# Random-feature attention and a low-rank mixer on one core: moving the weight loads, transposing the first tiles on TensorE, and pinning the order of loads

## The chip, the cores and the metric

The kernel runs on one core of a Trainium2 chip. The metric is the device time of one execution in microseconds (us). "Span" is the time from the first to the last instruction in a profiled execution; it is about 2 us shorter than the device time of the same execution. An execution counts as slow when it is over 1.5% above the fastest of the same kernel in its list, else as fast; ratios use fast ones alone.

## The reference, cut to what matters

Eight batches, eight heads, 576 positions, head size 64. Queries and keys are projected on 128 random directions; cosine and sine of the projections are the features. The attention is linear in those features. Its output x goes through a low-rank mix over the positions and then through a two-layer MLP of width 2048.

```python
def phi(x):
    proj = np.einsum('bhsd,md->bhsm', x, omega)
    return np.concatenate([np.cos(proj), np.sin(proj)], axis=-1) / np.sqrt(m)
kv  = np.einsum('bhsm,bhsd->bhmd', phi(k), v);  z = phi(k).sum(axis=2)
num = np.einsum('bhsm,bhmd->bhsd', phi(q), kv); den = np.einsum('bhsm,bhm->bhs', phi(q), z)
x   = num / den                                   # heads side by side: (8, 576, 512)
u   = x + (x.transpose(0, 2, 1) @ U @ V).transpose(0, 2, 1)
out = u + np.maximum(u @ w_ch1, 0) @ w_ch2
```

## The kernel before

Work is cut into 16 quads of four heads. A quad's k and q are loaded as bf16 by GpSimd's DMA queue, transposed by DMA on SyncE's queue, and used as two groups of two heads. A step s of the main loop emits the angles of group s, the key-values and numerators of group s-1, and one quarter of an MLP batch, six steps behind. A scheduler then places the instructions on the engines, a list for each. One point carries most of this study: an instruction that waits holds up those behind it on the same engine (in e8 below, a load on GpSimd that waits 6.7 us holds up the add behind it, and ScalarE with it).

A batch's 576 positions are four tiles of 128 and 64 left over. The leftovers of two batches, a pair, share one tile and are worked on together as the pair's tail, so the run has four pairs.

```python
    def load_quad(n, parts=1, veng=nc.sync):
        for name, src in (("k", k), ("q", q)):
            raw[name, n] = rawp.tile([P, 2, NS * D], BF16, name=f"{name}raw")
        vraw = rawp.tile([P, 2, NS * D], F32, name="vraw")
        # ... the k and q loads on nc.gpsimd, in parts
        veng.dma_start(vraw, quad(v, n))
        nc.gpsimd.tensor_copy(vq[n % NV][:, :, 0:D], vraw.rearrange("p i (s d) -> p (i s) d", d=D))
    # transpose_quad(n): nc.sync.dma_start_transpose(tpos[...], raw[...]) for k and q

    def angles(g):
        # ... TensorE: pk, pt, pq; VectorE turns them to integer angles `ang`
        for a in range(2):
            nc.scalar.activation(out=ft[:, 0, a, :], in_=low[:, a, :, 0], func=ACT.Sin, scale=TO_RAD)
            nc.gpsimd.tensor_scalar(out=ang[:, a, :], in0=ang[:, a, :], scalar1=TURN / 4.0,
                                    scalar2=1.0, op0=ALU.add, op1=ALU.mult)
        for a in range(2):
            nc.scalar.activation(out=ft[:, 1, a, :], in_=low[:, a, :, 0], func=ACT.Sin, scale=TO_RAD)
    # ... key_values(g), numerators(g); token_mix(b): hu, hn, u, then a DMA transpose u -> uT
    # ... channel_in: h_ps = W1 x uT, hid = relu(h_ps) on ScalarE; channel_out: ch_ps = hid x W2

    load_quad(0, parts=2, veng=nc.scalar)
    transpose_quad(0, parts=2)
    load_quad(1, veng=nc.scalar)
    load_low_rank()
    for a in range(4):
        load_w1(a)                      # 4 x 1 MB of HBM, on GpSimd's queue
    for s in range(NG + 6):
        if s % 2 == 0:
            n = s // 2
            if n + 2 < NG // 2:
                load_quad(n + 2)
            if n + 1 < NG // 2:
                transpose_quad(n + 1)
        if s == 1:
            for a in range(4):
                load_w2(a)
        if s < NG:
            angles(s)
        if 0 <= s - 1 < NG:
            key_values(s - 1)
            numerators(s - 1)
            if (s - 1) % 4 == 3:
                token_mix((s - 1) // 4)
        if s >= 6:
            b, mc = divmod(s - 6, 4)
            if b < B:
                mlp_chunk(b, mc)
```

`ang`: GpSimd's "quarter-turn add" on it turns the angle of a sine into that of a cosine, and the second pair of ScalarE activations waits for it.

Of the kernel before, what the change touches and what calls it, by code (L numbers as in the profile page):

```python
# [20 lines left out]
R = 32  # L21
# [18 lines left out]
TO_RAD = float(np.nextafter(np.float32(np.pi / 32768.0), np.float32(0.0)))  # L40


@with_exitstack
def kernel(
    ctx: ExitStack,
# [13 lines left out]
    const = ctx.enter_context(tc.tile_pool(name="const", bufs=1))  # L59
    stage = ctx.enter_context(tc.tile_pool(name="stage", bufs=1))  # L60
    rawp = ctx.enter_context(tc.tile_pool(name="rawp", bufs=2))
    tposp = ctx.enter_context(tc.tile_pool(name="tposp", bufs=2))
    angp = ctx.enter_context(tc.tile_pool(name="angp", bufs=3))
    featp = ctx.enter_context(tc.tile_pool(name="featp", bufs=3))
    kvp = ctx.enter_context(tc.tile_pool(name="kvp", bufs=2))
    xp = ctx.enter_context(tc.tile_pool(name="xp", bufs=2))
    up = ctx.enter_context(tc.tile_pool(name="up", bufs=2))
    hidp = ctx.enter_context(tc.tile_pool(name="hidp", bufs=2))
    outp = ctx.enter_context(tc.tile_pool(name="outp", bufs=3))
    smallp = ctx.enter_context(tc.tile_pool(name="smallp", bufs=4))  # L70
    psum = ctx.enter_context(tc.tile_pool(name="psum", bufs=2, space=bass.MemoryType.PSUM))


    ident = const.tile([P, P], BF16, name="ident")
    make_identity(nc, ident)
    om_f = stage.tile([P, 2, D], F32, name="om_f")
    nc.sync.dma_start(om_f, omega.unsqueeze(1).to_broadcast([P, 2, D]))
    om_b = stage.tile([P, 2, D], BF16, name="om_b")
    nc.vector.tensor_copy(om_b, om_f)
    wt_ps = psum.tile([P, P], BF16, name="wt_ps", tag="at")  # L80
    nc.tensor.transpose(wt_ps, om_b, ident)
    WT = const.tile([P, M], BF16, name="WT")
    nc.vector.tensor_copy(WT, wt_ps)

    Ub = const.tile([P, NT, R], BF16, name="Ub")
    Ut = const.tile([P, R], BF16, name="Ut")
    Vb = const.tile([P, S], BF16, name="Vb")

    def load_low_rank():
        U_f = stage.tile([P, NT + 1, R], F32, name="U_f")  # L90
        U9 = moe_U.rearrange("(p s) r -> p s r", s=NS)
        for e in range(2):
            r = slice(e * TL, (e + 1) * TL)
            nc.scalar.dma_start(U_f[r, 0:NT, :], U9[:, e:2 * NT:2, :])
            nc.scalar.dma_start(U_f[r, NT, :], U9[:, 8, :])
        nc.any.tensor_copy(Ub, U_f[:, 0:NT, :])
        nc.any.tensor_copy(Ut, U_f[:, NT, :])
        Vf = stage.tile([P, S], F32, name="Vf")
        for g in range(4):
            nc.scalar.dma_start(Vf[g * R:(g + 1) * R, :], moe_V)  # L100
        nc.any.tensor_copy(Vb.rearrange("r (s p) -> r s p", p=TL), Vf.rearrange("r (p s) -> r s p", s=NS))

    W1b = const.tile([P, 4, NCT, 512], BF16, name="W1b")
    W2b = const.tile([P, NFT, C], BF16, name="W2b")

    def load_w1(a):
        nc.gpsimd.dma_start(W1b[:, a, :, :],
                            moe_w_ch1[:, a * 512:(a + 1) * 512].rearrange("(c p) f -> p c f", p=P))

    def load_w2(a):  # L110
        nc.gpsimd.dma_start(W2b[:, 4 * a:4 * a + 4, :],
                            moe_w_ch2[a * 512:(a + 1) * 512, :].rearrange("(f p) c -> p f c", p=P))

    def w1(ct, f):
        return W1b[:, f // 4, ct, f % 4 * P:(f % 4 + 1) * P]
# [3 lines left out]
    for i in range(NV):  # L119
        a = const.tile([P, 2 * NS, D + 1], BF16, name=f"vq{i}")  # L120
        nc.vector.memset(a[:, :, D:D + 1], 1.0)
        vq.append(a)


    raw, tpos = {}, {}

    def quad(src, n):
        b, h0 = n // 2, 4 * (n % 2)
        return src[b, h0:h0 + 4, :, :].rearrange("(i e) (p s) d -> (e p) i (s d)", e=2, s=NS)

    def load_quad(n, parts=1, veng=nc.sync):
        for name, src in (("k", k), ("q", q)):
            raw[name, n] = rawp.tile([P, 2, NS * D], BF16, name=f"{name}raw")
        vraw = rawp.tile([P, 2, NS * D], F32, name="vraw")
        for i in range(parts):
            w = slice(i * 2 // parts, (i + 1) * 2 // parts)
            for name, src in (("k", k), ("q", q)):
                nc.gpsimd.dma_start(raw[name, n][:, w, :], quad(src, n)[:, w, :])  # L138
        veng.dma_start(vraw, quad(v, n))
        nc.gpsimd.tensor_copy(vq[n % NV][:, :, 0:D], vraw.rearrange("p i (s d) -> p (i s) d", d=D))  # L140

    def transpose_quad(n, parts=1):
        for name in ("k", "q"):
            tpos[name, n] = tposp.tile([P, NS, P], BF16, name=f"{name}T")
        cut = [0, NS] if parts == 1 else [0, 5, NS]
        for a, e in zip(cut, cut[1:]):
            for name in ("k", "q"):
                src = raw[name, n].rearrange("p i e -> p (i e)")
                nc.sync.dma_start_transpose(tpos[name, n][:, a:e, :], src[:, a * P:e * P])


    st, x_of = {}, {}
# [43 lines left out]
    def key_values(g):  # L196
        n, i = divmod(g, 2)
        ft = st[g]
        kv_ps = psum.tile([P, 2, 512], F32, name="kv_ps", tag="mm" if g < 4 else "at")
        for f in range(2):  # L200
            o = slice(f * (D + 1), (f + 1) * (D + 1))
            for s in range(NS):
                c = (s % 2 * 4 + s // 2) * M if s < 8 else 1024
                for hh in range(2):
                    r = slice(hh * TL, (hh + 1) * TL)
                    nc.tensor.matmul(kv_ps[:, hh, o], ft[r, f, 0, c:c + M], vq[n % NV][r, NS * i + s, :],  # L206
                                     start=(s == 0), stop=(s == NS - 1))
        kvb = kvp.tile([P, 2, 2, D + 1], BF16, name="kvb")
        nc.vector.tensor_copy(kvb.rearrange("p h f d -> p h (f d)"), kv_ps[:, :, 0:2 * (D + 1)])  # L209
        st[g] = (ft, kvb)  # L210
# [40 lines left out]
    def token_mix(b):  # L251
# [13 lines left out]
        for a in range(2):  # L265
            h_ps = psum.tile([P, 2, C], F32, name="hn", tag="at")
            for t in range(2):
# [3 lines left out]
        nc.tensor.matmul(h_ps[r, :], Vb[:, SM:S], hu)  # L271
        nc.vector.tensor_tensor(out=ut[r, :], in0=h_ps[r, :], in1=xt[r, :], op=ALU.add)
        uT = up.tile([P, NT, NCT, P], BF16, name="uT")
        nc.sync.dma_start_transpose(uT.rearrange("p t c s -> p (t c) s"),
                                    u.rearrange("p t c -> p (t c)"))
        u_of[b] = (u, uT)
        if b % 2 == 1:
            x_of.pop(("tail", b // 2))
# [60 lines left out]
    def mlp_chunk(b, mc):  # L339
        if mc == 0:  # L340
            channel_in(b, range(0, 8))
        elif mc == 1:
            channel_in(b, range(8, 16))
        elif mc == 2:
            channel_out(b, (0, 1))
            if b % 2 == 1:
                channel_in_tail(b // 2)
        else:
            channel_out(b, (2, 3))
            if b % 2 == 1:  # L350
                channel_out_tail(b // 2)
            u_of.pop(b)
            hid_of.pop(b)


    load_quad(0, parts=2, veng=nc.scalar)
    transpose_quad(0, parts=2)
    load_quad(1, veng=nc.scalar)
    load_low_rank()
    for a in range(4):  # L360
        load_w1(a)
    for s in range(NG + 6):
        if s % 2 == 0:
            n = s // 2
            if n + 2 < NG // 2:
                load_quad(n + 2)
            if n + 1 < NG // 2:
                transpose_quad(n + 1)
        if s == 1:
            for a in range(4):  # L370
                load_w2(a)
        if s < NG:
            angles(s)
        if 0 <= s - 1 < NG:
            key_values(s - 1)
            numerators(s - 1)
            if (s - 1) % 4 == 3:
                token_mix((s - 1) // 4)
        if s >= 6:
            b, mc = divmod(s - 6, 4)  # L380
            if b < B:
                mlp_chunk(b, mc)


# [28 lines left out]
```

## Time and profile before

| | before |
|---|---|
| median of the three runs at hand | 462.46 us (462.45 to 464.69) |
| span of the profiled execution (its device time was 470.2 us) | 468.0 us |
| TensorE busy | 368.2 us (79%) |
| first MLP matmul (h_ps) starts | 76.7 us |
| from there to the end | 391.3 us |

These are lines of the page of the kernel before: the span in 40 slices of 11.7 us, each digit the busy share in tenths; the second line is the DMA engines.

```profile
PE   0042266869997999879986999779989998999996
...
DMA  9999999651945266622964284413630511023022
```

For the first seven slices the DMA engines are at 90% or more; after that TensorE is busy for 60% or more of every slice. So the run has two parts, the head up to the first h_ps, and the rest. The chain of waits (start, duration, what; the longest pieces between 10 and 80 us) says what the head is made of:

```profile
14.14 14.04 DMA kT<-kraw
...
37.10 15.59 DMA qT<-qraw
...
70.35 6.35 DMA uT<-u
76.74 1.44 PE h_ps L295 x3
```

The second half of the first quad's kT takes 14.0 us from issue to landing, and the third quad's qT 15.6, where the medians of the run are 4.8 and 4.7. The list of waits of TensorE (us in total, times, longest, in the lists of other engines too) gives the sums:

```profile
PE h_ps L295 <- ACT hid L297: 26.9, 24, 3.4
PE pk L171 <- DMA kT<-kraw: 25.2, 3, 15.2
PE pt L176 <- DMA qT<-qraw: 10.3, 2, 6.8
```

```profile
POOL kraw L138 <- DMA kT<-kraw: 51.8, 9, 16.5
```

GpSimd (POOL) waits to reuse the buffer of a quad whose transpose has not landed.

### The profile page before, as it was taken

What the parts mean: (1) busy time and instruction counts of PE and PEld (TensorE: products, weight loads), DVE (VectorE), ACT (ScalarE), POOL (GpSimd) and SP (SyncE); (2) the same over time, 40 slices, a digit from 0 to 9 for tenths busy, and PEclk for the clock granted to TensorE, in tenths of its full rate; (3) what the DMA queues carried; (4) which work ended last, traced back from release to release, by engine and by line L of the source; (5) the groups of instructions that cost most, each with busy time, mean ns of one, the idle gap of its engine ahead of it and who ended that gap; (6) DMA issues with size and microseconds to landing.
All of it is one profiled execution on the core that took longest, in us unless ns stands there. A gap on an engine that the chain in (4) does not pass through costs nothing.

```text
span 468.0 us, 8400 instructions
## 1 busy us (share of the span) xinstructions
PE 368.2 (79%) x3572; PEld 186.2 (40%) x3601; DVE 196.7 (42%) x332; ACT 225.0 (48%) x275; POOL 121.1 (26%) x128
## 2 busy tenths in 40 slices
PE   0042266869997999879986999779989998999996
PEld 0022243424443554324433554334444544443452
DVE  1163355535535544336553534436644536251011
ACT  0355254863477443752476452762587147702520
POOL 7059233241324121321332231330221012100000
PEclk9999999979999999889999999989999999999999
DMA  9999999651945266622964284413630511023022
GB/s 220 218 221 142 222 224 173 102 87 57 176 119 101 61 138 114 116 37 77 154 148 74 67 153 93 77 27 59 117 74 1 79 37 45 0 59 90 0 47 67
DMA packets 81046, 47.66 MB, mean 102 GB/s; under 512 B 59888, under 2 KB 72176, under 8 KB 81008
## 3 DMA queue, kind: packets, MB, share of 16 engines
q1 hardware_dynamic: 66608, 31.93, 33.2%
q0 software_dynamic: 12960, 13.63, 19.9%
q10 hardware_dynamic: 1440, 1.56, 1.0%
q8 instruction: 28, 0.46, 0.4%
q14 instruction: 10, 0.08, 0.0%
HBM read 37.14 MB, written 9.44 MB: 100 GB/s over the span
## 4 chain that ended last, share of the span: by engine, by line
PE 52%; DMA 16%; ACT 13%; DVE 6%; POOL 6%; issue 4%; SPq 1%; another core or an unknown queue 0%; POOLq 0%; ACTq 0%
PE ch_ps L320 22%; PE h_ps L295 15%; DMA qT<-qraw 7%; DMA kT<-kraw 6%; ACT ft L193 5%; POOL ang L190 4%; ACT ft L189 4%; ACT hid L297 3%; PE ht_ps L308 3%; DVE ang L161 3%; PE ch_ps L332 3%; PE nd L228 3%; DMA kraw<-in_k_dram 1%; DMA uT<-u 1%; PE hn L268 1%
## 5 line engine op out<-in xcount | busy, mean ns | idle before, releaser
L295 PE MATMUL h_ps<-uT,W1b 128*128 128x512 bf16 x512 | 134.2, 399 | 31.2 <-ACT hid L297 26.9
L190 POOL TENSOR_SCALAR ang<-ang 128x1152 int32<-128x1152 int32 x64 | 73.3, 1153 | 197.9 <-ACT ft L189 176.1
L320 PE MATMUL ch_ps<-W2b,hid 128*128 128x512 bf16 x484 | 118.0, 379 | 3.7 <-ACT hid L297 1.5
L297 ACT ACTIVATE hid<-h_ps 128x512 bf16<-128x512 f32 x128 | 72.9, 591 | 72.0 <-PE h_ps L295 71.5
L189 ACT ACTIVATE ft<-ang 128x1152 bf16<-128x1152 int16 x64 | 73.8, 1160 | 65.0 <-DVE ang L161 51.3
L193 ACT ACTIVATE ft<-ang 128x1152 bf16<-128x1152 int16 x64 | 73.5, 1160 | 40.0 <-POOL ang L190 39.8
L295 PEld LDWEIGHTS <-W1b 128*128 128x128 bf16 x512 | 47.8, 101 | 87.0 <-issue 45.9
L320 PEld LDWEIGHTS <-hid 128*128 128x128 bf16 x512 | 46.8, 97 | 55.2 <-issue 5.0
L323 DVE TENSOR_TENSOR o<-ch_ps,u 128x512 f32<-128x512 f32 x32 | 21.9, 688 | 78.8 <-PE ch_ps L320 74.9
L161 DVE TENSOR_SCALAR ang<-pq 128x1024 int32<-128x1024 f32 x32 | 39.1, 1220 | 37.9 <-PE pq L181 37.9
L161 DVE TENSOR_SCALAR ang<-pk 128x1024 int32<-128x1024 f32 x32 | 39.0, 1219 | 31.4 <-PE pk L171 16.5
L171 PE MATMUL pk<-WT,kT 64*128 64x128 bf16 x256 | 15.9, 238 | 26.5 <-DMA kT<-kraw 25.2
L206 PEld LDWEIGHTS <-ft 64*128 64x128 bf16 x1152 | 24.5, 100 | 20.1 <-issue 14.9
L209 DVE CAST kvb<-kv_ps 128x260 bf16<-128x260 f32 x32 | 13.6, 423 | 40.2 <-PE kv_ps L206 40.2
L228 PE MATMUL nd<-kvb,ft 128*128 128x65 bf16 x512 | 23.6, 201 | 7.7 <-DVE kvb L209 7.6
L228 PEld LDWEIGHTS <-ft 128*128 128x128 bf16 x512 | 22.3, 103 | 17.4 <-issue 10.1
L310 ACT ACTIVATE hidt<-ht_ps 128x512 bf16<-128x512 f32 x16 | 9.5, 595 | 40.3 <-PE ht_ps L308 40.3
L138 POOL DMA_DIRECT2D kraw<-in_k_dram x17 | 12.2, 719 | 52.4 <-DMA kT<-kraw 51.8
L171 PEld LDWEIGHTS <-kT 64*128 64x128 bf16 x256 | 9.1, 102 | 40.2 <-DMA kT<-kraw 26.8
L239 DVE RECIPROCAL nd<-nd 128x10 f32<-128x10 f32 x32 | 7.3, 229 | 36.9 <-PE nd L234 36.9
L241 DVE TENSOR_TENSOR x<-nd,rec 128x512 bf16<-128x512 f32 x32 | 22.1, 692 | 1.1
L269 DVE TENSOR_TENSOR u<-hn,x 128x1024 bf16<-128x1024 f32 x16 | 18.8, 1220 | 6.1 <-PE hn L268 5.0
(56 smaller groups left out, 248.4 us busy)
## 6 DMA issues: line engine op xcount, KB each, us to landing
out_dram<-o SPq DMA_DIRECT2D x72, 128.0 KB, 2.4
vraw<-in_v_dram SPq DMA_DIRECT2D x14, 576.0 KB, 4.1
kraw<-in_k_dram POOLq DMA_DIRECT2D x15, 288.0 KB, 4.6
qraw<-in_q_dram POOLq DMA_DIRECT2D x15, 288.0 KB, 5.2
W1b<-in_moe_w_ch_dram POOLq DMA_DIRECT2D x4, 512.0 KB, 13.5
W2b<-in_moe_w_ch_dram POOLq DMA_DIRECT2D x4, 512.0 KB, 15.0
vraw<-in_v_dram ACTq DMA_DIRECT2D x2, 576.0 KB, 5.4
kraw<-in_k_dram POOLq DMA_DIRECT2D x2, 144.0 KB, 6.5
```

The costliest lines, as they stand in the source:

```text
L161: nc.vector.tensor_scalar(out=dst, in0=src, scalar1=TO_UNITS, scalar2=None, op0=ALU.mult)
L171: nc.tensor.matmul(pk[:, e, j * P:(j + 1) * P], kT[r, c, :], WT[r, :])
L189: nc.scalar.activation(out=ft[:, 0, a, :], in_=low[:, a, :, 0], func=ACT.Sin, scale=TO_RAD)
L190: nc.gpsimd.tensor_scalar(out=ang[:, a, :], in0=ang[:, a, :], scalar1=TURN / 4.0, scalar2=1.0, op0=ALU.add, op1=ALU.mult)
L193: nc.scalar.activation(out=ft[:, 1, a, :], in_=low[:, a, :, 0], func=ACT.Sin, scale=TO_RAD)
L206: nc.tensor.matmul(kv_ps[:, hh, o], ft[r, f, 0, c:c + M], vq[n % NV][r, NS * i + s, :], start=(s == 0), stop=(s == NS - 1))
L228: nc.tensor.matmul(nd[:, t // 2, 2 * (t % 2) + hh, :], ft[:, f, 1, c:c + P], kvb[:, hh, f, :], start=(f == 0), stop=(f == 1))
L241: nc.vector.tensor_tensor(out=x[:, :, hp * P:(hp + 1) * P].rearrange("p (a t) (h d) -> p a t h d", a=2, h=2), in0=nd[:, :, 0:4, 0:D], in1= ...
L295: nc.tensor.matmul(h_ps[:, f, :], w1(ct, f0 + f), uT[:, :, ct, :], start=(ct == 0), stop=(ct == NCT - 1))
L297: nc.scalar.activation(out=hid[:, f0 + f, :], in_=h_ps[:, f, :], func=ACT.Relu)
L320: nc.tensor.matmul(ch_ps, hid[:, f, t * P:(t + 1) * P], W2b[:, f, :], start=(f == 0), stop=(f == NFT - 1))
L323: nc.vector.tensor_tensor(out=o, in0=ch_ps, in1=u[:, t, :], op=ALU.add)
```

## The change

Its intent: keep the 8 MB of weights away from the first transposes, start the first angles earlier, and hand the engines a fixed order of loads.

```diff
-    tposp = ctx.enter_context(tc.tile_pool(name="tposp", bufs=2))
+    tposp = ctx.enter_context(tc.tile_pool(name="tposp", bufs=3))
-    hidp = ctx.enter_context(tc.tile_pool(name="hidp", bufs=2))
+    hidp = ctx.enter_context(tc.tile_pool(name="hidp", bufs=1))
+    def ordered(ins):
+        return tc.keep_in_program_order(ins)
     # load_quad no longer loads v; load_v(n) and widen_v(n) are separate;
     # k, q and v loads, v widenings and DMA transposes are wrapped in ordered(...)
+    def transpose_first():        # quad 0 on TensorE, in two rounds of blocks
+        ...
+                for c in blocks:
+                    nc.tensor.transpose(t_ps[:, j, c - blocks[0], :], src[:, c * P:(c + 1) * P], ident)
+                copy(out=tpos[name, 0][:, blocks[0]:blocks[-1] + 1, :], in_=t_ps[:, j, 0:len(blocks), :])
     # token_mix: uT by 16 TensorE transposes for b == 0, by DMA for b > 0
 # main part
+    load_quad(0, parts=2); make_identity(nc, ident); load_v(0); load_low_rank(); omega_t()
+    transpose_first(); load_quad(1); load_v(1); widen_v(0); load_quad(2)
     for s in range(NG + 6):
+        if s >= 6:                                   # the MLP chunk now opens the step
+            b, mc = divmod(s - 6, 4)
+            if b < B:
+                mlp_chunk(b, mc)
         ...                                          # loads, v, transposes, widen_v(n + 1)
+                gate = transpose_quad(n + 1)
+        if s == 4:
+            attend(3)                                # group 3 before the angles of group 4
         if s < NG:
             angles(s)
+        for a in {2: (0, 1), 3: (2, 3)}.get(s, ()):
+            w = ordered(load_w1(a))
+            if a == 0:
+                tc.add_manual_dep(w.ins, gate.ins.name, SYNC)
+        for a in {4: (0, 1), 5: (2, 3)}.get(s, ()):
+            ordered(load_w2(a))
+        if s != 4:
+            attend(s - 1)                            # key_values, numerators, token_mix
```

Smaller parts are cut here: the low-rank loads move to SyncE's queue and their casts to GpSimd, and a dummy sine preloads ScalarE's table.

More of the change, by code (lines that the diff above doesn't have):

```diff
@@ L40 @@
 TO_RAD = float(np.nextafter(np.float32(np.pi / 32768.0), np.float32(0.0)))
+SYNC = mybir.DependencyInfo(mybir.DependencyClass.Sync, mybir.DependencyReason.DATA)
 @with_exitstack
@@ L74, with omega_t @@
     ident = const.tile([P, P], BF16, name="ident")
-    make_identity(nc, ident)
     om_f = stage.tile([P, 2, D], F32, name="om_f")
     nc.sync.dma_start(om_f, omega.unsqueeze(1).to_broadcast([P, 2, D]))
-    om_b = stage.tile([P, 2, D], BF16, name="om_b")
-    nc.vector.tensor_copy(om_b, om_f)
-    wt_ps = psum.tile([P, P], BF16, name="wt_ps", tag="at")
-    nc.tensor.transpose(wt_ps, om_b, ident)
+    warm = stage.tile([P, 1], F32, name="warm")
+    nc.vector.memset(warm, 0.0)
+    nc.scalar.activation(out=warm, in_=warm, func=ACT.Sin)
     WT = const.tile([P, M], BF16, name="WT")
-    nc.vector.tensor_copy(WT, wt_ps)
+    def omega_t():
+        om_b = stage.tile([P, 2, D], BF16, name="om_b")
+        nc.vector.tensor_copy(om_b, om_f)
+        wt_ps = psum.tile([P, P], BF16, name="wt_ps", tag="at")
+        nc.tensor.transpose(wt_ps, om_b, ident)
+        nc.vector.tensor_copy(WT, wt_ps)
     Ub = const.tile([P, NT, R], BF16, name="Ub")
@@ L87 @@
     Vb = const.tile([P, S], BF16, name="Vb")
+    U_f = stage.tile([P, NT + 1, R], F32, name="U_f")
+    Vf = stage.tile([P, S], F32, name="Vf")
     def load_low_rank():
-        U_f = stage.tile([P, NT + 1, R], F32, name="U_f")
         U9 = moe_U.rearrange("(p s) r -> p s r", s=NS)
@@ L93, in load_low_rank, with cast_low_rank @@
             r = slice(e * TL, (e + 1) * TL)
-            nc.scalar.dma_start(U_f[r, 0:NT, :], U9[:, e:2 * NT:2, :])
-            nc.scalar.dma_start(U_f[r, NT, :], U9[:, 8, :])
-        nc.any.tensor_copy(Ub, U_f[:, 0:NT, :])
-        nc.any.tensor_copy(Ut, U_f[:, NT, :])
-        Vf = stage.tile([P, S], F32, name="Vf")
-        for g in range(4):
-            nc.scalar.dma_start(Vf[g * R:(g + 1) * R, :], moe_V)
-        nc.any.tensor_copy(Vb.rearrange("r (s p) -> r s p", p=TL), Vf.rearrange("r (p s) -> r s p", s=NS))
+            nc.sync.dma_start(U_f[r, 0:NT, :], U9[:, e:2 * NT:2, :])
+            nc.sync.dma_start(U_f[r, NT, :], U9[:, 8, :])
+        for g in range(4):
+            nc.sync.dma_start(Vf[g * R:(g + 1) * R, :], moe_V)
+    def cast_low_rank():
+        nc.gpsimd.tensor_copy(Ub, U_f[:, 0:NT, :])
+        nc.gpsimd.tensor_copy(Ut, U_f[:, NT, :])
+        nc.gpsimd.tensor_copy(Vb.rearrange("r (s p) -> r s p", p=TL), Vf.rearrange("r (p s) -> r s p", s=NS))
     W1b = const.tile([P, 4, NCT, 512], BF16, name="W1b")
@@ L106, in load_w1 @@
     def load_w1(a):
-        nc.gpsimd.dma_start(W1b[:, a, :, :],
-                            moe_w_ch1[:, a * 512:(a + 1) * 512].rearrange("(c p) f -> p c f", p=P))
+        return nc.gpsimd.dma_start(W1b[:, a, :, :],
+                                   moe_w_ch1[:, a * 512:(a + 1) * 512].rearrange("(c p) f -> p c f", p=P))
     def load_w2(a):
-        nc.gpsimd.dma_start(W2b[:, 4 * a:4 * a + 4, :],
-                            moe_w_ch2[a * 512:(a + 1) * 512, :].rearrange("(f p) c -> p f c", p=P))
+        return nc.gpsimd.dma_start(W2b[:, 4 * a:4 * a + 4, :],
+                                   moe_w_ch2[a * 512:(a + 1) * 512, :].rearrange("(f p) c -> p f c", p=P))
     def w1(ct, f):
@@ L129, in quad, with load_quad @@
         return src[b, h0:h0 + 4, :, :].rearrange("(i e) (p s) d -> (e p) i (s d)", e=2, s=NS)
-    def load_quad(n, parts=1, veng=nc.sync):
-        for name, src in (("k", k), ("q", q)):
+    def load_quad(n, parts=1):
+        for name in ("k", "q"):
             raw[name, n] = rawp.tile([P, 2, NS * D], BF16, name=f"{name}raw")
-        vraw = rawp.tile([P, 2, NS * D], F32, name="vraw")
         for i in range(parts):
@@ L137, in load_quad, with load_v, widen_v, transpose_quad @@
             for name, src in (("k", k), ("q", q)):
-                nc.gpsimd.dma_start(raw[name, n][:, w, :], quad(src, n)[:, w, :])
-        veng.dma_start(vraw, quad(v, n))
-        nc.gpsimd.tensor_copy(vq[n % NV][:, :, 0:D], vraw.rearrange("p i (s d) -> p (i s) d", d=D))
-    def transpose_quad(n, parts=1):
+                ordered(nc.gpsimd.dma_start(raw[name, n][:, w, :], quad(src, n)[:, w, :]))
+    def load_v(n):
+        raw["v", n] = rawp.tile([P, 2, NS * D], F32, name="vraw")
+        ordered(nc.sync.dma_start(raw["v", n], quad(v, n)))
+    def widen_v(n):
+        ordered(nc.gpsimd.tensor_copy(vq[n % NV][:, :, 0:D],
+                                      raw.pop(("v", n)).rearrange("p i (s d) -> p (i s) d", d=D)))
+    def transpose_quad(n):
         for name in ("k", "q"):
             tpos[name, n] = tposp.tile([P, NS, P], BF16, name=f"{name}T")
-        cut = [0, NS] if parts == 1 else [0, 5, NS]
-        for a, e in zip(cut, cut[1:]):
-            for name in ("k", "q"):
-                src = raw[name, n].rearrange("p i e -> p (i e)")
-                nc.sync.dma_start_transpose(tpos[name, n][:, a:e, :], src[:, a * P:e * P])
+            last = ordered(nc.sync.dma_start_transpose(tpos[name, n], raw.pop((name, n)).rearrange("p i e -> p (i e)")))
+        return last
+    def transpose_first():
+        for name in ("k", "q"):
+            tpos[name, 0] = tposp.tile([P, NS, P], BF16, name=f"{name}T")
+        for blocks in (range(0, 4), range(4, NS)):
+            t_ps = psum.tile([P, 2, 8, P], BF16, name="t_ps", tag="mm")
+            for j, (name, copy) in enumerate((("k", nc.vector.tensor_copy), ("q", nc.scalar.copy))):
+                src = raw[name, 0].rearrange("p i e -> p (i e)")
+                for c in blocks:
+                    nc.tensor.transpose(t_ps[:, j, c - blocks[0], :], src[:, c * P:(c + 1) * P], ident)
+                copy(out=tpos[name, 0][:, blocks[0]:blocks[-1] + 1, :], in_=t_ps[:, j, 0:len(blocks), :])
     st, x_of = {}, {}
@@ L273, in token_mix @@
         uT = up.tile([P, NT, NCT, P], BF16, name="uT")
-        nc.sync.dma_start_transpose(uT.rearrange("p t c s -> p (t c) s"),
-                                    u.rearrange("p t c -> p (t c)"))
+        if b > 0:
+            nc.sync.dma_start_transpose(uT.rearrange("p t c s -> p (t c) s"),
+                                        u.rearrange("p t c -> p (t c)"))
+        else:
+            for a in range(2):
+                t_ps = psum.tile([P, 2, NCT * 2, P], BF16, name="t_ps", tag="mm")
+                for t in range(2):
+                    for ct in range(NCT):
+                        nc.tensor.transpose(t_ps[:, t, ct, :], u[:, 2 * a + t, ct * P:(ct + 1) * P], ident)
+                    copy = nc.scalar.copy if t == 0 else nc.vector.tensor_copy
+                    copy(out=uT[:, 2 * a + t, :, :], in_=t_ps[:, t, 0:NCT, :])
         u_of[b] = (u, uT)
@@ L353, in mlp_chunk, with attend @@
             hid_of.pop(b)
-    load_quad(0, parts=2, veng=nc.scalar)
-    transpose_quad(0, parts=2)
-    load_quad(1, veng=nc.scalar)
+    load_quad(0, parts=2)
+    make_identity(nc, ident)
+    load_v(0)
     load_low_rank()
-    for a in range(4):
-        load_w1(a)
-    for s in range(NG + 6):
-        if s % 2 == 0:
-            n = s // 2
-            if n + 2 < NG // 2:
-                load_quad(n + 2)
-            if n + 1 < NG // 2:
-                transpose_quad(n + 1)
-        if s == 1:
-            for a in range(4):
-                load_w2(a)
-        if s < NG:
-            angles(s)
-        if 0 <= s - 1 < NG:
-            key_values(s - 1)
-            numerators(s - 1)
-            if (s - 1) % 4 == 3:
-                token_mix((s - 1) // 4)
+    omega_t()
+    transpose_first()
+    load_quad(1)
+    load_v(1)
+    widen_v(0)
+    load_quad(2)
+    gate = None
+    def attend(g):
+        if 0 <= g < NG:
+            key_values(g)
+            numerators(g)
+            if g % 4 == 3:
+                token_mix(g // 4)
+    for s in range(NG + 6):
         if s >= 6:
@@ L382 @@
                 mlp_chunk(b, mc)
+        if s == 0:
+            transpose_quad(1)
+        if s % 2 == 0:
+            n = s // 2
+            if 3 <= n + 2 < NG // 2:
+                load_quad(n + 2)
+            if n + 2 < NG // 2:
+                load_v(n + 2)
+            if 2 <= n + 1 < NG // 2:
+                gate = transpose_quad(n + 1)
+            if n + 1 < NG // 2:
+                widen_v(n + 1)
+        if s == 1:
+            cast_low_rank()
+        if s == 4:
+            attend(3)
+        if s < NG:
+            angles(s)
+        for a in {2: (0, 1), 3: (2, 3)}.get(s, ()):
[6 more added lines that the diff above has]
+            attend(s - 1)
 _INS = ['q', 'k', 'v', 'omega', 'moe_U', 'moe_V', 'moe_w_ch1', 'moe_w_ch2']
```

## The prediction

> **What bounds it now.** A starved head, then a TensorE-bound rest. In the windows table TensorE is busy about 16 of the first 75 us, and 285 of the 320 us from 120 to 440 (89%). The first MLP matmul (h_ps) starts at 76.7 us; from there to the end are 391 us, cut by the ends of the pair tails into 105.5, 105.4, 99.2 and 81.2 us. The head is DMA: about 200 to 250 GB/s until 75 us. The 4 MB of W1 are issued at 9.2 us, W2 at 33.9 us, amid the DMA transposes: kT takes 14.0 us from issue to landing (median over the run 4.8), qT of the third quad 15.6. The chain of waits shows both; the waits list has TensorE 25.2 us on kT, 10.3 us on qT. TensorE runs in order and pk/pt of the third quad stand before the key-values of the second, so 37.8 to 52.7 us is nearly empty although MLP batch 0 did not need that data. All these queues share engines (the Trainium skill, "DMA: Bandwidth & Descriptors", section "Issuing engines are not separate DMA queues"); the slow transposes agree.
>
> **What changes.**
> - First quad: 18 TensorE transposes and four PSUM copies for four DMA transposes. Eight 128x128 matmuls take 0.61 us here, so about 2 us plus copies of about 0.7 us (estimate from 128x512 casts of 0.69). kraw lands near 9 us, so the first angles are complete near 14 us instead of 26.5.
> - W1 waits for the third quad's transposes, W2 for steps 4 and 5: no 4 MB load beside the transposes of quads 1 and 2. I expect those to land in 5 to 8 us each.
> - Instruction order (read from the build): groups 0 to 3 and token mix 0 now precede the third quad's angles on TensorE; the 15 us hole goes. First u: 16 TensorE transposes, about 3 us instead of 6.35.
> - Against it: GpSimd's fixed order puts widen_v(1), the low-rank casts, widen_v(2) and the gated W1 issue ahead of quarter-turn adds. I expect group 0's adds near 20 us and group 3's near 38, so MLP starts near 51 us rather than the 44 that ScalarE (4 activations of 1.16 us per group) would allow. W1 and W2 now compete with quad 3 and 4 transposes: up to 5 us of TensorE stall after the MLP start.
> - Steady state: one hid buffer, transposes one buffer deeper, MLP emitted first. uT has 6 to 12 us of matmuls to hide behind instead of 11 to 34, against a 4.8 us landing plus 2.4 us of adds. Work is unchanged, so 388 to 396 us from MLP start to end.
>
> **Sum.** 51 + 391 + 2 = 444 us of span against 468, all on the critical path since everything after the first h_ps is TensorE-bound: 462.5 - 25 is about 437 us. Range 428 to 446. Chances: faster by over 2% 0.95, within 2% 0.04, slower 0.01.
>
> **What would show it.** First pk near 10 us; kT/qT of quads 1 and 2 landing in under 9 us; no qT wait over 5 us before MLP 0; first h_ps between 45 and 56 us; W1 issued at 30 to 40 us; pair periods within 3% of before; TensorE busy total within 2%.
>
> **What would make it wrong.** GpSimd blocked on the gate so long that group 3 is late (h_ps after 58 us); W1 or W2 landing late (h_ps or ch_ps waiting on DMA); the new order opening bubbles at every batch (pairs over 109 us), because uT or hid are waited for; or, on the other side, a tighter steady state with pairs under 102 us.

## The result, and the profile after

The changed kernel took 430.56 us (median of four runs, 428.27 to 431.39); the kernel before 463.57 (median of four, 462.45 to 469.14). Ratios here are the mean time of one kernel's fast runs over that of the other's of the same rounds, so not quite the ratio of these medians: 0.926, with a 95% interval of 0.917 to 0.934. The profiled execution spans 426.4 us.

The same lines of the page of the changed kernel (slices of 10.7 us now):

```profile
PE   3476888978899989978899989978899979979995
...
DMA  9999995689148680679147580687515410142013
```

TensorE works from the first slice and is busy at 70% or more from the fifth slice to the last but one. Its waits, and in the second fence GpSimd's:

```profile
PE h_ps L329 <- ACT hid L331: 12.6, 20, 1.0
PE nd L253 <- DVE kvb L234: 7.2, 17, 0.6
...
PE ch_ps L354 <- DVE o L357: 3.9, 5, 2.2
PE ht_ps L342 <- ACT hidt L344: 3.5, 7, 0.7
...
PE pk L196 <- DMA kT<-kraw: 3.0, 1, 3.0
```

```profile
POOL ang L215 <- ACT ft L214: 235.8, 49, 13.4
POOL vq_110 L156 <- DMA vraw<-in_v_dram: 3.4, 1, 3.4
```

TensorE's 35 us on kT and qT are down to 3. GpSimd has no wait on kT at all. Its large first line is only the engine having nothing to do until ScalarE is done with `ang`. The h_ps wait on ScalarE has halved.

Cutting every trace at the first h_ps and at the start of the VectorE add that ends each pair tail gives the table that the rest of this text uses. Each row is one profiled execution; "rest" is from the first h_ps to the end.

| kernel | first h_ps | pair 1 | pair 2 | pair 3 | pair 4 | rest | span |
|---|---|---|---|---|---|---|---|
| before | 76.7 | 105.6 | 105.4 | 99.1 | 76.7 | 391.3 | 468.0 |
| before, second profile (e1) | 78.9 | 106.5 | 101.6 | 99.5 | 76.7 | 388.8 | 467.7 |
| changed | 45.0 | 99.8 | 96.4 | 98.1 | 82.2 | 381.4 | 426.4 |

Two things stand out. About three quarters of the 41.6 us between the spans lie in the head (76.7 - 45.0 = 31.7), and 9.9 us lie in the rest. And pair 4 got longer, by 5.5 us.

Two cautions. The cuts do not hold the same work. Before its first h_ps the kernel before has run the angles of six groups and the key-values of five (48 pk and 180 kv_ps matmuls), the changed kernel those of five and four (40 and 144). So about 2 us of the head's gain (an estimate from the mean busy times per group) is work that moved into the rest. Pair 4 of the changed kernel in turn holds one group of attention more (144 kv_ps matmuls against 108), which is about half of its 5.5 us: TensorE is busy there for 74.8 us, against 72.3 in e1. The other caution: the profiled execution of the kernel before was a long one (470.2 us), so the 41.6 us are more than the 33 us between the medians of the result; where those 8 us lie is not known.

### The profile page after: what moved, and what is told of

The parts are those of the page before. It is cut to its first block, busy times and chain, and to the rows that moved or that the text cites. A ratio compares the mean times of both kernels' runs of the same rounds, so it can differ in the third digit from the quotient of the medians.

```text
span 426.4 us, 8512 instructions
## 1 busy us (share of the span) xinstructions
PE 366.4 (86%) x3635; PEld 187.1 (44%) x3635; DVE 198.5 (47%) x335; ACT 225.3 (53%) x278; POOL 123.2 (29%) x131
## 4 chain that ended last, share of the span: by engine, by line
PE 53%; ACT 20%; DVE 9%; POOL 7%; issue 6%; DMA 3%; POOLq 0%; ACTq 0%; DVEq 0%
PE ch_ps L354 22%; PE h_ps L329 15%; ACT ft L214 7%; ACT ft L218 7%; POOL ang L215 6%; ACT hid L331 5%; DVE ang L186 4%; PE ch_ps L366 3%; PE ht_ps L342 3%; PE nd L253 2%; DVE u L294 2%; DMA uT<-u 1%; DMA kraw<-in_k_dram 1%; PE hn L293 1%; ACT hidt L344 1%
## 5 line engine op out<-in xcount | busy, mean ns | idle before, releaser
L329 PE MATMUL h_ps<-uT,W1b 128*128 128x512 bf16 x512 | 123.3, 382 | 14.9 <-ACT hid L331 12.6
L354 PE MATMUL ch_ps<-W2b,hid 128*128 128x512 bf16 x512 | 123.3, 383 | 3.9 <-DVE o L357 3.9
L253 PEld LDWEIGHTS <-ft 128*128 128x128 bf16 x512 | 21.7, 101 | 17.4 <-ACT ft L218 6.9
L234 DVE CAST kvb<-kv_ps 128x260 bf16<-128x260 f32 x32 | 13.5, 423 | 21.2 <-PE kv_ps L231 21.1
L342 PE MATMUL ht_ps<-utT,W1b 128*128 128x128 bf16 x256 | 16.9, 219 | 3.5 <-ACT hidt L344 3.5
L186 DVE TENSOR_SCALAR ang<-pt 128x256 int32<-128x256 f32 x32 | 13.4, 418 | 12.8 <-PE pt L201 12.4
```

The lines of the kernel that those rows point to most:

```text
L186: nc.vector.tensor_scalar(out=dst, in0=src, scalar1=TO_UNITS, scalar2=None, op0=ALU.mult)
L253: nc.tensor.matmul(nd[:, t // 2, 2 * (t % 2) + hh, :], ft[:, f, 1, c:c + P], kvb[:, hh, f, :], start=(f == 0), stop=(f == 1))
L329: nc.tensor.matmul(h_ps[:, f, :], w1(ct, f0 + f), uT[:, :, ct, :], start=(ct == 0), stop=(ct == NCT - 1))
L342: nc.tensor.matmul(h_ps[:, a, f, :], w1(ct, f0 + 4 * a + f), utT[:, ct, :], start=(ct == 0), stop=(ct == NCT - 1))
L354: nc.tensor.matmul(ch_ps, hid[:, f, t * P:(t + 1) * P], W2b[:, f, :], start=(f == 0), stop=(f == NFT - 1))
```

## The experiments

All kernels below gave correct results. Where no profile is quoted, the figures are from the profiled execution of the run. "Before" means runs of the kernel before on the same chip in the same rounds. In the three calls those medians were 469.7, 471.2 and 470.0 us, so somewhat above the 462.5 that the prediction started from. The gain: 33 us in the result above, 42 us for e5, which has the changed kernel's order (429.2 against 471.2).

**e1, the kernel before once more.** No edit.

> The kernel before, unchanged, for a second profile, because its first profile (span 468.0 us) was longer than its timed runs (462.5). If the profile is typical: span 460 to 469, first h_ps near 76 us, the first two pairs near 105 us and the third near 99, GpSimd's kraw issue waiting about 50 us in total on kT landing. If the first profile was an odd one (throttling near 100 us), the pairs will come out some us shorter and the head alone will account for nearly all of the 33 us gain.

Measured: 470.2 us (468.6 to 472.2), span 467.7, first h_ps 78.9 us, GpSimd's kraw issue waiting 49.9 us on kT. The first profile was typical in shape. Only pair 2 differs (101.6 against 105.4), so a part of the 9.9 us of the rest, up to some 3 us, is variation of the kernel before. This run was 1.2% slower than the other runs of the very same kernel in its call (ratio 1.012, interval 1.000 to 1.024). The ratio leaves out the runs that count as slow against the fastest of their own list, and here one list has a fastest run of 462.0 and the other of 468.6; the medians of all runs are 470.2 and 469.7. Differences of about 1% between kernels built on the one before settle nothing.

**e2, a third transpose buffer alone,** on the kernel before.

```diff
-tposp bufs=2, hidp bufs=2
+tposp bufs=3, hidp bufs=1
```

> The kernel before with three transpose buffers and one hid buffer, nothing else. Theory A: after the head, the gain comes from the third transpose buffer, which lets transposes leave early so that GpSimd's kraw issue no longer waits on kT landing: that wait falls from about 52 us to under 25, pairs one and two fall from 105 to about 100 us, the time falls by 6 to 10 us to 452 to 457. Rival B: it comes from the new emission order (MLP first), so this one stays at 460 to 465.

Measured: 468.4 us, ratio to before 1.006 (0.990 to 1.023). The total wait of GpSimd's kraw issue on kT fell only to 42.2 us, and 17.9 us on qT appeared. First h_ps came at 83.9 us, 5 us later than in e1; the rest was 385.3 us (388.8 in e1), pairs 1 to 3 105.9, 102.5 and 95.8. Theory A as stated fails. Whether the third buffer helps the rest of the kernel before a little and costs as much in its head is more than one profile can say.

**e3, two transpose buffers again,** in the changed kernel (the order of instructions on every engine is then identical).

```diff
-tposp bufs=3
+tposp bufs=2
```

> The changed kernel with two transpose buffers again; the instruction order of every engine stays as it is in the changed kernel. Theory A: GpSimd waits on kT landing again (tens of us), pair periods rise from 97 to above 101 us, time 436 to 441. Rival B: time stays within 1% of 430.6 (at most 434).

Measured: 430.2 us (428.9 to 430.9), ratio 0.926, the same as the changed kernel. GpSimd still does not wait on kT. In the changed kernel the third transpose buffer neither gives nor costs anything that can be seen. The hid buffer stayed at one here, so its count was not tested in the changed kernel.

**e4, the weights early again,** in the changed kernel.

```diff
     load_v(1)
+    for a in range(4): ordered(load_w1(a))
     widen_v(0)
 ...  # and no W1, W2 loads in steps 2 to 5, no gate
         if s == 1:
             cast_low_rank()
+            for a in range(4): ordered(load_w2(a))
```

> The changed kernel with W1 issued right after the second quad's loads and W2 in step 1, as before, ungated; all else of the change kept. Theory C (weights beside the transposes make the slow head): kT and qT of the second and third quad land in over 10 us, first h_ps moves from 45 to 55 us or later, time 438 to 446. Rival D (the order of the instructions gives the head's gain, the weights little): h_ps before 50 us and time at most 434.

Measured: 447.6 us (445.7 to 449.7), 17 us above the changed kernel and above e3 of the same rounds (430.2). First h_ps is at 62.2 us, and the rest is 381.6 us, the same as the changed kernel's 381.4. So the whole 17 us is head. kT of the second and third quad landed in 12.6 and 16.2 us (7.4 and 7.9 in the changed kernel), and TensorE's waits on them are back (list of waits of TensorE in e4):

```profile
PE pk L196 <- DMA kT<-kraw: 8.3, 1, 8.3
...
PE pt L201 <- DMA qT<-qraw: 6.3, 1, 6.3
```

Theory C holds: within the changed kernel, the place of the weights is worth 17 us.

**e5, without the gate.** The changed kernel without the semaphore wait of the first W1 load.

```diff
             w = ordered(load_w1(a))
-            if a == 0:
-                tc.add_manual_dep(w.ins, gate.ins.name, SYNC)
```

> The changed kernel without the semaphore wait of the first W1 load on the third quad's transposes; the instruction order is the same on every engine. In the profile of the changed kernel W1 is issued at 28.6 us, when GpSimd comes out of the quarter-turn adds, so program order alone may hold it there. If so: W1 issued between 27 and 30 us, time within 1% of 430.6. If the gate is what holds W1: issue several us earlier, the third quad's transposes land later, time 433 or more.

Measured: 429.2 us (428.1 to 430.7), first h_ps at 46.0. The gate does nothing here. GpSimd's timeline in the changed kernel (start, duration, engine, line, operation) shows why:

```profile
25.26 1.17 POOL L156 CAST vq_112<-vraw 128x1152 bf16<-128x1152 f32 x1
26.39 2.27 POOL L215 TENSOR_SCALAR ang<-ang 128x1152 int32<-128x1152 int32 x2
28.60 1.53 POOL L116 DMA_DIRECT2D W1b<-in_moe_w_ch_dram  x2
30.15 2.28 POOL L215 TENSOR_SCALAR ang<-ang 128x1152 int32<-128x1152 int32 x2
```

W1 is issued the moment GpSimd comes out of its adds, with no idle time in front. It is program order on GpSimd that holds the weights back; the third quad's transposes have already landed by then (qT at 27.4 us).

**e6, only the weights late,** in the kernel before.

```diff
-    for a in range(4): load_w1(a)            # before the loop
-        if s == 1: for a in range(4): load_w2(a)
         if s < NG: angles(s)
+        for a in {2: (0, 1), 3: (2, 3)}.get(s, ()): load_w1(a)
+        for a in {4: (0, 1), 5: (2, 3)}.get(s, ()): load_w2(a)
```

> The kernel before with only the weight loads moved: W1 in steps 2 and 3, W2 in steps 4 and 5, no gate. Theory C (weights make the slow head): transposes of quads 0 to 2 land in under 9 us, first h_ps moves from 76.7 to 55 to 62 us, time 443 to 450. Rival D (order): h_ps stays above 70 us, time above 456.

Measured: 473.4 us against 471.2 for before; three of its four runs, the profiled one included, count as slow against its fastest (463.0), so no ratio is given. Neither expectation was right in its mechanism. The edit did not move everything: the scheduler still issued one of the four W1 loads at 8.2 us, beside the first quad's transposes. The transposes of the second quad did land in 3.4 us (those of the third took 7.5 and 13.5), and token mix finished at about 56 us instead of 70. But first h_ps stayed at 79.2 us (list of waits of TensorE in e6):

```profile
PE h_ps L295 <- ACT hid L297: 27.2, 24, 3.9
PE h_ps L295 <- DMA uT<-u: 19.3, 1, 19.3
PE pk L171 <- DMA kT<-kraw: 14.5, 1, 14.5
```

The weights now ran beside the next DMA transposes in line, that of the first u among them, which took 22.8 us from issue to landing. The collision had moved by some 20 us and cost as much in its new place. This holds for this slow profile. Its three slow runs (473.4 to 475.8 us) show no gain either; its one fast run, 463.0, is 6 us below the fastest of the kernel before in that call (468.9), so a small gain stays possible.

**e12, late weights and the first u on TensorE,** both in the kernel before: e6 plus the 16 TensorE transposes of the change.

```diff
+        if b > 0:
             nc.sync.dma_start_transpose(uT.rearrange("p t c s -> p (t c) s"), u.rearrange("p t c -> p (t c)"))
+        else: ...   # two rounds of TensorE transposes with PSUM copies, as in the change
```

> The kernel before with the late weights of e6, and in addition the first u transposed on TensorE. In e6 TensorE waited 19.3 us for the DMA transpose of that u, which ran beside the late weights. If late weights need this to pay: first h_ps at 58 to 63 us instead of 79, time 12 to 18 us below the kernel before of the same call. If the weights or quad 3 then hold it up instead: gain under 6 us.

Measured: 458.9 us (453.9 to 460.3) against 470.0, ratio 0.977 (0.968 to 0.985). First h_ps is at 57.4 us, 21.5 us earlier than in e1. About 11 us of that remain, a little under the expected 12: pair 1 became 113.2 us, and GpSimd still waits 45.3 us on kT. The timelines of GpSimd, ScalarE and TensorE show how one such wait is passed on:

```profile
72.82 0.70 POOL L138 DMA_DIRECT2D kraw<-in_k_dram  x1 [10.81 <-DMA kT<-kraw]
73.54 2.27 POOL L190 TENSOR_SCALAR ang<-ang 128x1152 int32<-128x1152 int32 x2
```

```profile
74.73 2.27 ACT L193 ACTIVATE ft<-ang 128x1152 bf16<-128x1152 int16 x2 [13.57 <-POOL ang L190]
```

```profile
77.54 1.01 PE L304 MATMUL h_ps<-uT,W1b 128*128 128x512 bf16 x2 [13.33 <-ACT hid L306]
```

So late weights, which alone showed no clear gain, pay together with the first u on TensorE (that part alone, with early weights, was not run); and the time that the head gains can be lost right behind it. As in e6, one of the four W1 loads still went out early, at 8.0 us.

**e7, the first quad by DMA,** in the changed kernel.

```diff
-    transpose_first()
+    transpose_quad(0)
```

> The changed kernel with the first quad transposed by DMA again (one transpose each for k and q), not on TensorE. If the TensorE transposes are worth what the prediction said: first angles 6 to 9 us later, first h_ps at 50 to 54 us instead of 45, time 436 to 440. If GpSimd's wait for the second v load hides them: h_ps moves by under 3 us, time at most 434.

Measured: 432.6 us (431.1 to 433.5), against 429.2 for e5 in the same rounds, which has the changed kernel's order. First h_ps is at 48.8 us instead of 46.0. The 18 TensorE transposes are worth about 3 us (up to 0.7 us of them the gate, which e7 has and e5 has not), not the 12.8 us by which the first angles came forward against the kernel before (13.7 after 26.5). With the weights away, the first quad's DMA transposes took only 5.8 and 4.4 us, and the second quad's kT landed at 18.7 us, hardly later than in the changed kernel (18.4).

**e8, GpSimd's wait for the second v moved.** In the changed kernel GpSimd waits 3.35 us for the second v load before the first quarter-turn add. The widening goes behind those adds; the low-rank casts are emitted a step later, too, but the scheduler still places them first.

```diff
-            if n + 1 < NG // 2:
+            if n + 1 < NG // 2 and s > 0:
                 widen_v(n + 1)
-        if s == 1:
+        if s == 2:
             cast_low_rank()
 ...
             angles(s)
+        if s == 1:
+            widen_v(1)
```

> The changed kernel with one GpSimd instruction moved: the widening of the second quad's v goes behind the quarter-turn adds of groups 0 and 1; every other engine's order is the same. In the changed kernel GpSimd waits 3.35 us for that load and ScalarE then waits 3.38 us for the adds. If that wait is on the critical path: first adds near 13.5 us instead of 17.1, first h_ps 2 to 4 us earlier (41 to 43), time 426.5 to 428.5, faster than the changed kernel by 0.5 to 1%. If kT of the second quad (landing at 18.5 us) is the next limit: under 1 us gained.

Measured: 434.9 us (433.4 to 437.8), slower than e5 of the same rounds by 5.7 us. The first half of the expectation came true: the first add starts at 13.3 us instead of 17.1. Then this happens (the timelines of GpSimd, ScalarE and SyncE in e8; in brackets the idle time before and what ended it):

```profile
34.84 1.52 POOL L116 DMA_DIRECT2D W1b<-in_moe_w_ch_dram  x2 [6.72 <-DMA qT<-qraw]
36.38 1.17 POOL L215 TENSOR_SCALAR ang<-ang 128x1152 int32<-128x1152 int32 x1
```

```profile
37.58 1.16 ACT L218 ACTIVATE ft<-ang 128x1152 bf16<-128x1152 int16 x1 [6.55 <-POOL ang L215]
```

```profile
17.39 4.37 SPq L153 DMA_DIRECT2D vraw<-in_v_dram  x2
21.86 2.13 SPq L162 DMA_TRANSPOSE kT<-kraw  x1
```

The same two lines of SyncE's timeline in the changed kernel:

```profile
17.41 1.05 SPq L153 DMA_DIRECT2D vraw<-in_v_dram  x2
18.55 2.33 SPq L162 DMA_TRANSPOSE kT<-kraw  x1
```

GpSimd reached the gated W1 load at 28.1 us, hardly earlier than in the changed kernel (28.6). But the gate, the landing of the third quad's qT, now opened at 34.6 us instead of 27.4, and held GpSimd for 6.7 us in front of the last add of group 3. The moved widening frees the buffer of the second quad's v; it ended at 21.4 us, and only then did SyncE issue its next v load, with the third quad's transposes behind it. First h_ps slipped to 50.8 us. This is the risk that the prediction named, GpSimd blocked on the gate; it did not bite in the changed kernel because the transposes landed 1.2 us before GpSimd came.

**e9, e8 without the gate.**

> The run with the moved v widening (e8), now without the W1 wait on the third quad's transposes. If e8 lost time only because the gate held GpSimd (6.7 us) in front of group 3's last quarter-turn add: W1 issued near 28 us, the last add done near 31 us, first h_ps at 42 to 44.5 us, time 426 to 429, the fastest so far or level with it. If e8 lost it because the second quad's v and the later loads came later: h_ps stays at 48 us or more, time 432 or more.

Measured: 432.6 us (430.0 to 436.8; its three fast runs lie between 430.0 and 433.6), and a profile in the slow state. First h_ps is at 44.9 us, near the expected range, so the gate did hold up the head in e8; but pair 1 is 107.5 us instead of 99.8. The third quad's kT was still issued late (22.4 us), W1 from 26.6 us now ran beside the third quad's transposes, the fourth quad's qT took 19.7 us to land, and TensorE met the collision behind the first h_ps (its timeline):

```profile
59.46 0.26 PE L201 MATMUL pt<-qT,WT 64*128 64x128 bf16 x1 [5.82 <-DMA qT<-qraw]
```

Not all of pair 1's 7.7 us is that wait: TensorE is idle there for 14.9 us instead of 9.9, and busy for 92.6 instead of 89.9, with more h_ps and ch_ps matmuls that took over 450 ns (17 instead of 6). What holds from the timed runs is that removing the wait at 14.5 us gains nothing that can be seen.

**e11, without pinning,** in the changed kernel: the scheduler places loads, widenings and transposes freely. The gate stays.

```diff
     def ordered(ins):
-        return tc.keep_in_program_order(ins)
+        return ins
```

> The changed kernel without the pinning of loads, v widenings and transposes to program order; the scheduler places them freely, as before. Rival E (pinned order keeps GpSimd from waiting in front of the quarter-turn adds): GpSimd waits on kT landing for 20 us or more again, first h_ps to end rises to 386 or more, time above 434. Theory B: it stays at 380 to 384 after the first h_ps, and only the head may change.

Measured: 461.5 us (459.7 to 463.4) against 470.0 for before, ratio 0.984 (0.977 to 0.991). Of the 31 us that are lost against the changed kernel's 430.6 (not of the same call, where e10 took 417.8), the head takes 9.7 (first h_ps at 54.7) and pair 1 takes 18.0 (117.8 us); pairs 2 and 3 are at 98.1 each. GpSimd's waits (the list of e11) look like those of the kernel before:

```profile
POOL kraw L149 <- DMA kT<-kraw: 51.9, 8, 13.0
POOL qraw L149 <- DMA qT<-qraw: 9.5, 3, 7.6
POOL W1b L116 <- DMA qT<-qraw: 6.2, 1, 6.2
```

and ScalarE's wait on the quarter-turn adds is 58.8 us, against 32.0 in the changed kernel. Rival E is right about the head and the first pair, and says too much about the later pairs. Of the 51.9 us, 27.9 lie in pair 1, where TensorE is idle for 23.0 us (9.9 in the changed kernel), and 23.3 in pair 2, where it is idle for 8.7 us, as in the changed kernel: there the wait cost TensorE nothing. Since the gate stayed in and now blocks for 6.2 us, the 31 us are the price of free order with this gate, not of free order alone.

**e10, the MLP chunk at the end of the step,** as before, in the changed kernel.

```diff
     for s in range(NG + 6):
-        if s >= 6: ...mlp_chunk(b, mc)
 ...
         if s != 4:
             attend(s - 1)
+        if s >= 6: ...mlp_chunk(b, mc)
```

> The changed kernel with the MLP chunk emitted at the end of each step, as before, instead of the start. In the profiles so far the time from first h_ps to the end is 385 to 392 us in the kernels built on the one before and 380 to 385 in those built on the changed one. Theory B (emission order gives this part): it rises to 386 or more and time to 434 or more. Rival E (the fixed order of loads on GpSimd and SyncE gives it): it stays at 380 to 384, time 428 to 432.

Measured: 417.8 us (417.75 to 418.27), ratio to before 0.891 (0.884 to 0.898). Both theories were wrong: emitting the MLP first had not given anything, it had cost something. This kernel beats both, the changed one by 2 to 3% (417.8 over 430.6; they did not run in the same call, but e5, with the changed kernel's order, stands at 0.912 of before in its call, interval 0.908 to 0.915). First h_ps is at 46.0 us, as in e5, and the rest is 370.0 us instead of 381.4. The first fence is TensorE's line of this run's page, the second from its list of waits:

```profile
PE   3476888998899989998999989999899989999995
```

```profile
PE h_ps L329 <- ACT hid L331: 13.6, 21, 1.2
PE nd L253 <- DVE kvb L234: 5.4, 17, 0.6
...
PE ht_ps L342 <- ACT hidt L344: 0.7, 1, 0.7
```

The rows of the table that belong to the experiments:

| kernel | us, median | first h_ps | pair 1 | pair 2 | pair 3 | pair 4 | rest |
|---|---|---|---|---|---|---|---|
| e4, weights early | 447.6 | 62.2 | 99.8 | 96.4 | 98.1 | 82.5 | 381.6 |
| e5, no gate | 429.2 | 46.0 | 99.8 | 96.4 | 96.4 | 82.8 | 380.2 |
| e10, MLP last | 417.8 | 46.0 | 101.1 | 93.9 | 93.9 | 76.3 | 370.0 |
| e11, unpinned | 461.5 | 54.7 | 117.8 | 98.1 | 98.1 | 84.0 | 403.2 |
| e12, late weights and first u | 458.9 | 57.4 | 113.2 | 100.7 | 99.8 | 76.4 | 394.7 |

The MLP-last kernel saves 2.5 and 4.2 us in pairs 2 and 3, and 4.6 us in pairs 1 and 4 taken together (with the order, one group of attention moves from pair 4 into pair 1). The gain is idle time and not faster matmuls: in the rest TensorE is busy for 343.0 us (341.7 in the changed kernel) and idle for 27.1 (39.7). The sum of all listed waits of TensorE is 53.9 us in the changed kernel and 41.7 us here. The waits that went are of one kind, short ones at the seams between MLP and attention: ch_ps on the VectorE add of the previous tile (3.9 us, now none), ht_ps on ScalarE (3.5 to 0.7), hn and pk on the u adds (5.4 to 1.4), and uT (1.0, now none). Why the scheduler leaves those seams when the MLP comes first was not taken apart.

## Why the prediction was right, and where its terms were off

The time, 430.6 us, lies in the range of 428 to 446; the gain was larger than the 25 us of the sum. Some of this is luck. The sum was 444 us of span where 426.4 were measured, too long by 17.6 us. It was compared with the span of an execution of 470.2 us, but the difference was taken off the median of 462.5; taken off 470.2, a range as wide would have been 436 to 454 and have missed. The terms follow.

- **The starved head.** Right. e4 puts 17 us on the place of the weights. kT and qT of quads 1 and 2 landed in 5.9 to 7.9 us, as said (under 9). The Trainium skill's "DMA: Bandwidth & Descriptors", section "Issuing engines are not separate DMA queues", says that DMAs from all issuing engines run on the same 16 DMA engines and interleave; e4 against the changed kernel puts a number to it here, 12.6 and 16.2 us for kT with the weights beside it, 7.4 and 7.9 without.
- **"51" for the MLP start** was mis-sized: it measured 45.0. I had group 0's adds near 20 us (17.1 measured) and group 3's near 38 (30.2 measured), because I took the gate to hold W1 until the third quad's transposes landed at some later time. W1 was issued at 28.6 us with no wait, and e5 shows the gate free. The mechanism is real, as e8 shows with 6.7 us, only not binding here.
- **The first quad on TensorE.** The first angles were complete at 13.7 us, as said (14). What I did not say is how little that is worth: e7 measures about 3 us, for with the weights away the DMA transposes of that quad are short too (5.8 and 4.4 us).
- **The third quad's hole and the first u.** Right in that the 15 us hole is gone; the reason given, the order of instructions, is not shown. In e12, with late weights and the old order, TensorE's two waits for the third quad are down to one of 2.2 us (7.4 and 6.8 in the kernel before), so late weights alone close most of it. The new order was not tried alone. e6 and e12 show that TensorE transposes for the first u are not a small saving (3 us rather than 6.35) but what lets late weights pay clearly; with them moved late and the transpose left on the DMA queue, it took 22.8 us.
- **"Up to 5 us of TensorE stall after the MLP start"**, of which 2 went into the sum: none showed in the changed kernel, where TensorE waits for DMA for 1.0 us in all after the first h_ps. The collision itself did move there: the fourth quad's kT and qT took 11.8 and 17.4 us beside W1, but TensorE had MLP work to do.
- **"388 to 396 us from MLP start to end, work is unchanged."** Mis-sized: 381.4. Two things changed against e1 (388.8 us; from the profile of the kernel before 28 ch_ps records are missing, so its busy time is not used). TensorE is busy for 341.7 us instead of 345.8, although one group's angles and key-values moved into the rest: 14 of its h_ps and ch_ps matmuls took over 450 ns instead of 33 (the usual is 379); why is not shown, and e3 with the same order has 25. And it is idle for 39.7 us instead of 43.0: the h_ps wait on ScalarE fell from 26.5 to 12.6 us, but other waits grew, those of the MLP-first order among them. GpSimd's wait on kT went from 49.9 us to none. I had that wait in my list and read it as a harmless load issue. e11 ties it to the pinned order, and its cost to the head and the first pair. For pairs 2 and 3, which stay at 98.1 us without pinning against 99 to 105 before, the cause is not settled: e3 rules the third transpose buffer out within the changed kernel, e2 leaves it open for the kernel before (pair 3 at 95.8); the hid buffer, the separate emission of the v widening and the other low-rank placement were not tried alone.
- **"MLP emitted first"** I took for neutral, with a tail risk of bubbles. It costs about 11 us (381.4 against 370.0), hidden under the gains from the rest of the change.
- **Signs.** Pairs were within 3% in pair 3 only; pairs 1 and 2 were 5 and 9% shorter, pair 4 was 7% longer. TensorE's busy total (366.4 against 368.2) was within 2%. W1 was issued at 28.6 us, before the 30 to 40 named, and first h_ps at 45.0 us, at the edge of 45 to 56. One sign that the prediction had named as showing it wrong came true: a tighter rest, with pairs 1 to 3 under 102 us.

## What to carry to other kernels

When a bulk load collides with transposes, look at what it will collide with in its new place before moving it; here late weights paid clearly only once the next transpose in line had left the DMA queues. Where an engine both issues DMA and computes, look at what stands behind every wait of such an issue: in e11 one part of GpSimd's wait went with 18 us of pair 1 and another, as long, cost nothing in pair 2. Pin the order if the scheduler puts such an issue in front of urgent work. And a widening that is moved also moves the moment at which its buffer comes free, and with it the loads and transposes behind (e8). Take a change of several parts apart even when it wins: one part of this one cost 11 us, and undoing it gave the best kernel.

## What the Trainium skill lacked or had wrong

- "DMA: Bandwidth & Descriptors", section "Issuing engines are not separate DMA queues", states the sharing but not what a transfer loses by it. Here the DMA transpose of u, 4.8 us at the median, took 22.8 us beside the weight loads (e6), and kT between 3.2 us and 21.2 us in that one kernel.
- "Advanced Engine Details and Errata", section "X-Bar Transpose (TRN2)", says that transpose DMAs are as fast as regular ones. The medians of the kernel before agree (kT 4.8 us; the load of the same tile 4.6 us, though it reads twice the bytes, in f32). What the section does not say is how both stretch in a crowded head: up to 14.0 us for kT and 18.3 us for kraw in the same kernel.
- "TensorE: Matmul & The Clock Gate", Part 4 on the PE-mode transpose, gives the duration of one (about 275 ns in context; in the changed kernel's trace 285 to 314 ns for the first quad's and 216 to 314 ns for those of u) and no rate for a run of them. Multiplying it by 18 would be wrong: the 18 transposes of the first quad took 2.66 us of TensorE's busy time (0.61 + 0.71 + 0.63 + 0.71).
- The same page, Part 1, section "Seeing it yourself", warns that a trace's clock events can't be fully trusted. Here it is the reading of them that needs care. The windows of the kernel before show a clock of 1.00 between 20 and 60 us, while the 64x512 matmuls of pq there took 609 ns at the median, against 387 ns between 60 and 400 us. But the first clock record of that trace stands at 81.9 us (41.6 us in the changed kernel), and the view counts time without a record as full clock. Where there is a record, the matmuls agree with it: from 284.0 to 287.4 us of the changed kernel the clock is 0.50 and the ch_ps matmuls take 634 ns at the median instead of 379. Before the first record, the matmul's own duration is the better witness.
